# Windowed attention and two gated layers: block 1 keeps block 0's two PSUM pools, and the shared ring of four banks opens one block later

## Chip, cores and metric

One core of one Trainium2 chip. The metric is the device time of a run in microseconds (us); lower is better. A run counts by the median of several.

## What is computed

```python
scores = (1/sqrt(64)) * q @ k.T                    # 4 batches, 8 heads, 576 positions, head size 64
mask   = (rel >= 0) & (rel < 64)                   # each position sees itself and the 63 before it
x      = softmax(where(mask, scores, -1e9)) @ v    # -> 2304 tokens x 512
h      = x @ w_in                                  # 512 -> 2048
y      = gate(h) @ w_out                           # 2048 -> 512
h2     = y @ w_in2                                 # 512 -> 1024
out    = layernorm(h2 * softmax(h2)) * g_ln @ w_out2   # 1024 -> 512
```

## The kernel before

The tokens go in six blocks of 384 (`NBLK`). In each block the first layer runs over 16 feature slices `f` of 128. For one slice `moe_h` (L496) makes `ps_h` with 12 matmuls of 384 columns (four chunks of the model width, three products each, since every operand is split into a high and a low part), ACT and DVE make the gated value in two parts (L505, L506, L511, L512, L515), and two steps later `moe_y` (L526) adds it to four accumulators `acc` with 12 more matmuls. At a block's end `moe_out` copies the accumulators to `xo` (L536 on ACT, L538 on DVE) and POOL stores them (L539).

Between these steps stands the attention of the next block, cut into pieces that `slot()` takes from the generator `slots()`, one or two in each step. Up to the start of block 1 a piece treats a group of two heads: `st_s` makes scores (L352, with masked maximum on DVE at L360 and exponential on ACT at L366), `st_norm` divides (L377 to L386), `st_t` transposes the weights (`ps_p`, L400 and L402, copied out on ACT at L405 and L407), `st_v` multiplies with v (`ps_x`, L421, taken out at L428 and L429). From the group pair `PU` on a piece treats four heads: `pair_s` fills two score banks (L442, with L452 and L458 behind it), then two transposed banks, and `pair_v` one bank `ps_x` (L476, L483, L484). The pieces of block 1 make the input of block 2, and so on.

PSUM has eight banks. Four hold the accumulators. The other four belong, up to the end of block 0, to two pools of two: `ps_at` for the attention's tiles and `ps_h` for the slices. Then both are closed and one pool of four, the ring, gives its banks in turn to whoever asks, attention or slice (`at_bank`, `h_bank`). The loop over `seq` near the end (L850 on) writes the program step by step, and there the switch is made. The kernel is recorded with a scheduler that reorders instructions within each engine, so the order on an engine follows from the dependences that the banks leave, not from the text alone.

```python
    def h_bank():
        if ring:
            return ring[0].tile([128, 512], F32, tag="r", name="ps_h")
        return ps_h.tile([128, 512], F32, tag="h", name="ps_h")
```

Of the kernel before, what the change touches and what calls it, by code (L numbers as in the profile page):

```python
# [20 lines left out]
def kernel(  # L21
# [73 lines left out]
    def at_bank(name):  # L95
        if spare:
            spare.append(spare.pop(0))
            if spare[-1] is not None:
                return ps_acc.tile([128, 512], F32, tag=spare[-1], name=name)
        if ring:  # L100
            return ring[0].tile([128, 512], F32, tag="r", name=name)
        return ps_at.tile([128, 512], F32, tag="a", name=name)
# [47 lines left out]
    def w_conv(start=True):  # L150
        if w_b:
            split_c(*w_b.pop(0))
        if w_a:
            w_b.append(w_a.pop(0))
            split_b(*w_b[-1])
        if w_raw and start:
            w_a.append(w_raw.pop(0))
            split_a(*w_a[-1])
# [72 lines left out]
    def w2_vals(k):  # L231
        for y, a in (("B1", 0), ("B2", 2)):
            z = d_p.tile([128, 2, 512], F32, tag="st", bufs=4, name="w2v")
            for c in range(2):
                nc.sync.dma_start(out=z[:, c, :], in_=w2d[2 * (k + a) + c])
                w2v[f"{y}{c + 1}", k] = z[:, c, :]

    def w2_sums(k):
        for tag, a, b in (("e", "T1", "T2"), ("s", "T3", "T4")):
            z = d_p.tile([128, 2, 512], F32, tag=tag, bufs=3, name="w2t")  # L240
            w2v[a, k], w2v[b, k] = z[:, 0, :], z[:, 1, :]
        for y, a, b in (("T1", "B12", "B11"), ("T2", "B22", "T1"), ("T3", "B22", "B12"), ("T4", "B21", "T2")):
            nc.gpsimd.tensor_tensor(w2v[y, k], w2v[a, k], w2v[b, k], op=ALU.subtract)
# [246 lines left out]
    def moe_h(j, f, c):  # L490
        ps = h_bank()[:, c]
        n = 0
        for kc in range(KC):
            hi, lo = wih[f][:, kc, :], wil[f][:, kc, :]
            for a, bb in ((hi, xh[j]), (hi, xl[j]), (lo, xh[j])):
                nc.tensor.matmul(ps, a, bb[:, kc, c], start=(n == 0), stop=(n == 3 * KC - 1))  # L496
                n += 1
        return ps

    def moe_g(part, ps):  # L500
        c = part[2]
        u = wk_p.tile([128, NB], F32, tag="u", name="u")[:, c]
        hi = wk_p.tile([128, NB], F32R, tag="gh", bufs=3, name="gh")[:, c]
        lo = wk_p.tile([128, NB], F32R, tag="gl", bufs=3, name="gl")[:, c]
        nc.scalar.activation(u, ps, ACTF.Relu, bias=half, scale=0.5)  # L505
        nc.scalar.activation(u, u, ACTF.Square)  # L506
        gh[part[0], part[1], part[2].start], gl[part[0], part[1], part[2].start] = hi, lo
        return ps, u, hi, lo

    def moe_g2(ps, u, hi, lo):  # L510
        g = nc.vector.scalar_tensor_tensor(u, u, 1.0, ps, op0=ALU.min, op1=ALU.max)  # L511
        return nc.scalar.copy(hi, u).ins, g.ins  # L512

    def moe_g3(j, ps, u, hi, lo):
        nc.vector.tensor_tensor(lo, u, as_f32(hi), op=ALU.subtract)  # L515


    def moe_y(j, f, c):
        if f == 0 and c.start == 0:
            for e in range(KC):  # L520
                acc[j, e] = ps_acc.tile([128, 512], F32, tag=f"acc{e}", bufs=1, name=f"acc{e}")
        hi, lo = gh.pop((j, f, c.start)), gl.pop((j, f, c.start))
        for e in range(KC):
            wh, wl = woh[f][:, e * 128:(e + 1) * 128], wol[f][:, e * 128:(e + 1) * 128]
            for n, (a, bb) in enumerate(((wh, hi), (wh, lo), (wl, hi))):
                nc.tensor.matmul(  # L526
                    acc[j, e][:, c], a, bb,
                    start=(f == 0 and n == 0 and c.start == 0), stop=(f == NF - 1 and n == 2),
                )

    def moe_out(j, es):
        for e in es:
            xo = wk_p.tile([128, NB], F32, tag="u" if j == NBLK - 1 and e > 1 else "xo", name="xo")
            a = acc.pop((j, e))[:, 0:NB]
            if e % 2 == 0:
                nc.scalar.copy(xo, a)  # L536
            else:
                nc.vector.tensor_copy(xo, a)  # L538
            nc.gpsimd.dma_start(out=x2d[j][e], in_=xo)  # L539
# [9 lines left out]
    def w_load(n=1):  # L549
        for _ in range(n):  # L550
            if wq:
                w_raw.append(w1_unit(*wq.pop(0)))
# [96 lines left out]
    def slot(n):  # L649
        for _ in range(n):  # L650
            next(stages, None)
# [7 lines left out]
    def x2_load(p):  # L659
        r = x2r[p] = d_p.tile([128, KC, 256], F32, tag="x2", bufs=2, name="x2r")  # L660
        c = 0
        while c < 256:
            j, c0 = divmod(256 * p + c, NB)
            n = min(256 - c, NB - c0)
            nc.sync.dma_start(out=r[:, :, c:c + n], in_=x2d[j][:, :, c0:c0 + n].rearrange("e p n -> p e n"))
            c += n
# [171 lines left out]
    def l2_norm(m):  # L838
        ln_pins.append(st_ln(m))
        st_move(m)  # L840
# [9 lines left out]
    for n in range(len(seq) + 2):  # L850
        if n < len(seq):
            j, f, c = seq[n]
            last = j == NBLK - 1
            n0 = n1 = 1
            if c == FIRST:
                z = na * (f + 1) // F0 - na * f // F0
                n0, n1 = z - z // 2, z // 2
            if j == 1 and f == 0:
                fr_ctx.close()
                ring.append(rg_ctx.enter_context(  # L860
                    tc.tile_pool(name="ps_ring", bufs=4, space=PSUM, reuse_waits="tile")
                ))
            if last and f == 8:
                rg_ctx.close()
                ring[0] = ps_ctx.enter_context(tc.tile_pool(name="ps_ring2", bufs=2, space=PSUM, reuse_waits="tile"))
            if last and f == 0:
                at_ctx.close()
                d_p = ctx.enter_context(tc.tile_pool(name="d", bufs=2, side="right", reuse_waits="tile"))
                x2_load(0)
            if j == 1 and f == 4:  # L870
                gl_row = wk_p.tile([128, NB], F32, tag="xo", name="gl_row")[0:DF2 // 128, 0:128]
                nc.sync.dma_start(
                    out=gl_row.rearrange("k (b i) -> k b i", b=4),
                    in_=g_ln.rearrange("(b k i) -> k b i", b=4, i=32),
                )
            if j == 1 and f == 7:
                ps = at_bank("ps_g")
                nc.tensor.transpose(ps[:, 0:DF2 // 128], gl_row, ident[0:DF2 // 128, 0:DF2 // 128])
                nc.vector.tensor_copy(gl_sb, ps[:, 0:DF2 // 128])
            part = moe_g(seq[n], moe_h(j, f, c))  # L880
        if n >= 1 and n - 1 < len(seq):
            moe_g3(seq[n - 1][0], *prev)
        if n < len(seq):
            prev = part
            slot(n0)
            w_conv()
            pins = moe_g2(*part)
        if n >= 2:
            jy, fy, cy = seq[n - 2]
            moe_y(jy, fy, cy)  # L890
            if fy == NF - 1:
                moe_out(jy, (0, 1))
        if n < len(seq):
            slot(n1)
            w_conv()
            if j == 0:
                w_load(2)
            w2_step(n, *pins)
            if last and f < 2:
                w2_vals(f)  # L900
            if last and f in (2, 3):
                w2_sums(f - 2)
            if last and f >= 2:
                with tc.issue_after(pins[0]):
                    w2_split(f - 2)
            if last and 2 <= f < 10:
                w2_load(f - 2)
        else:
            w_conv()
        if n >= 2 and fy == NF - 1:  # L910
            moe_out(jy, (2, 3))
        if n < len(seq):
            if last and f == 1:
                x2_load(1)
            if last and f == 5:
                with tc.issue_after(pins[0]), tc.issue_after(pins[1]):
                    x2_prep(0)
            if last and f in P_STEPS:
                st_p(0, P_STEPS[f])
            if last and f == 14:  # L920
                l2_norm(0)
            if last and f == 15:
                st_p(1, "P2")
        elif n == len(seq):
            x2_load(2)
            x2_prep(1)
            st_p(1, "P3")
            l2_norm(1)
# [66 lines left out]
```

## Time and profile before

| | |
|---|---|
| median of 3 runs | 703.74 us (703.43 to 706.93) |
| profiled execution: its own time | 703.17 us |
| profiled execution: span from first to last instruction | 701.4 us |
| PE (matmul) busy | 678.1 us, 97% of the span |
| PEld (weight load) busy | 625.6 us, 89% |
| DVE busy | 448.3 us, 64% |
| ACT busy | 412.5 us, 59% |
| POOL busy | 134.2 us, 19% |

The span lies within the execution's own time, 1.8 us less. Busy time of PE counts overlapping matmuls once, and ends of matmuls are modelled, so a busy PE can still be slowed. The granted clock of TensorE is 0.998 of full speed over the span.

### The profile page before, as it was taken

Reading aid. Unit: us, or ns where it says so; the run is one execution under the profiler, and the core shown is the slowest. Engines: PE = TensorE matmul, PEld = TensorE weight load, DVE = VectorE, ACT = ScalarE, POOL = GpSimd, SP = SyncE. Lnnn points to the kernel's source line nnn. Section 1 sums busy time; section 2 is a strip of 40 time slices with the busy share of each in tenths; the row PEclk is TensorE's granted clock in tenths of the full one; section 3 lists DMA queues with packets and bytes.
Section 4 is the critical chain, followed back from the end, with each engine's and each line's share of the span. In section 5 each row is a group of like instructions: output and inputs, shape, how many; then the busy total and the mean of one; then the engine's idle time right before and its main releaser. Section 6 shows DMA issues by size and latency. Waiting matters only on the chain.

```text
span 701.4 us, 12574 instructions
## 1 busy us (share of the span) xinstructions
PE 678.1 (97%) x4439; PEld 625.6 (89%) x4439; DVE 448.3 (64%) x1213; ACT 412.5 (59%) x1006; POOL 134.2 (19%) x178
## 2 busy tenths in 40 slices
PE   6899888899999999999999999999999999999998
PEld 5689788799999999999999999999997888888887
DVE  4789889646445555454455552643289999999850
ACT  5889777665656655665566565364455555445451
POOL 1112221100001000021112111662272322220000
PEclk9999999999999999999999999999999999999999
DMA  9996896625353523346351211562024455444331
GB/s 194 253 241 161 218 245 196 148 35 108 72 116 112 116 64 76 77 129 126 85 113 61 106 41 51 173 202 93 1 83 142 155 178 189 158 147 150 103 109 46
DMA packets 150551, 88.94 MB, mean 127 GB/s; under 512 B 118616, under 2 KB 134744, under 8 KB 150488
## 3 DMA queue, kind: packets, MB, share of 16 engines
q1 hardware_dynamic: 135160, 49.84, 30.2%
q0 software_dynamic: 12592, 33.57, 14.9%
q10 hardware_dynamic: 2736, 4.72, 1.8%
q8 instruction: 35, 0.57, 0.3%
q14 instruction: 28, 0.23, 0.1%
HBM read 63.97 MB, written 24.12 MB: 126 GB/s over the span
## 4 chain that ended last, share of the span: by engine, by line
PE 71%; issue 13%; POOL 4%; DVE 4%; DMA 3%; SPq 3%; ACT 2%; POOLq 0%; DVEq 0%
PE acc L526 21%; PE ps_h L496 21%; PE ps_o L827 14%; PE P L712 9%; DMA wst<-in_moe_w_in_dram 3%; POOL wil L249 2%; PE ps_x L476 2%; PE ps_s L442 2%; PE ps_p L402 2%; SPq L279 1%; DVE gl L515 1%; POOL wst L124 1%; SPq L302 1%; POOL wst L126 1%; DVE x2p L692 1%
## 5 line engine op out<-in xcount | busy, mean ns | idle before, releaser
L511 DVE SCALAR_TENSOR_TENSOR u<-u,ps_h 128x384 f32<-128x384 f32 (+1 forms) x98 | 53.3, 544 | 142.3 <-ACT u L506 141.4
L496 PE MATMUL ps_h<-xh,wih 128*128 128x384 f32 (+1 forms) x392 | 132.0, 337 | 3.1 <-ACT wih L145 3.0
L526 PE MATMUL acc<-gl,woh 128*128 128x384 f32 (+1 forms) x392 | 130.3, 334 | 2.1 <-DVE gl L515 2.1
L496 PE MATMUL ps_h<-xl,wih 128*128 128x384 f32 (+1 forms) x392 | 130.7, 334 | 0.4 <-DVE xl L429 0.4
L496 PE MATMUL ps_h<-xh,wil 128*128 128x384 f32 (+1 forms) x392 | 130.9, 334 | 0.0
L526 PE MATMUL acc<-gh,wol 128*128 128x384 f32 (+1 forms) x392 | 129.3, 332 | 0.0
L526 PE MATMUL acc<-gh,woh 128*128 128x384 f32 (+1 forms) x392 | 123.8, 341 | 2.3 <-ACT gh L512 2.3
L505 ACT ACTIVATE u<-ps_h,half 128x384 f32<-128x384 f32 (+1 forms) x98 | 56.1, 574 | 97.5 <-PE ps_h L496 97.3
L515 DVE TENSOR_TENSOR gl<-u,gh 128x384 fp32r<-128x384 f32 (+1 forms) x98 | 62.6, 640 | 35.2 <-ACT gh L512 34.6
L512 ACT CAST gh<-u 128x384 fp32r<-128x384 f32 (+1 forms) x98 | 49.7, 508 | 49.9 <-DVE u L511 34.8
L496 PEld LDWEIGHTS ps_h<-xh,wih 128*128 128x128 f32 x392 | 74.1, 189 | 4.5 <-ACT wih L145 3.6
L526 PEld LDWEIGHTS acc<-gh,woh 128*128 128x128 f32 x392 | 72.0, 188 | 6.2 <-ACT gh L512 3.5
L526 PEld LDWEIGHTS acc<-gl,woh 128*128 128x128 f32 x392 | 73.7, 188 | 3.1 <-DVE gl L515 2.7
L496 PEld LDWEIGHTS ps_h<-xl,wih 128*128 128x128 f32 x392 | 74.1, 189 | 1.0 <-DVE xl L429 0.8
L496 PEld LDWEIGHTS ps_h<-xh,wil 128*128 128x128 f32 x392 | 74.1, 189 | 0.1
L526 PEld LDWEIGHTS acc<-gh,wol 128*128 128x128 f32 x392 | 73.6, 188 | 0.1
L712 PE MATMUL P<-wih,x2p 128*128 128x512 f32 x216 | 71.6, 390 | 0.7 <-DVE x2p L692 0.7
L827 PE MATMUL ps_o<-woh,wol 128*128 128x512 f32 (+1 forms) x152 | 57.6, 379 | 0.0
L827 PE MATMUL ps_o<-woh,woh 128*128 128x512 f32 (+1 forms) x152 | 57.5, 379 | 0.0
L827 PE MATMUL ps_o<-wol,woh 128*128 128x512 f32 (+1 forms) x152 | 57.5, 378 | 0.0
L506 ACT ACTIVATE u<-u 128x384 f32<-128x384 f32 (+1 forms) x98 | 51.1, 522 | 1.9
L712 PEld LDWEIGHTS P<-wih,x2p 128*128 128x128 f32 x216 | 40.4, 188 | 9.2 <-DVE x2p L692 1.1
(123 smaller groups left out, 1191.8 us busy)
## 6 DMA issues: line engine op xcount, KB each, us to landing
wst<-in_moe_w_out_dram POOLq DMA_DIRECT2D x22, 512.0 KB, 7.4
wst<-in_moe_w_in_dram POOLq DMA_DIRECT2D x21, 512.0 KB, 5.5
vw<-in_v_dram SPq DMA_DIRECT2D x32, 256.0 KB, 5.3
lnd<-e SPq DMA_DIRECT2D x16, 512.0 KB, 2.7
lT<-lnd SPq DMA_DIRECT2D x64, 128.0 KB, 3.0
x2d<-xo POOLq DMA_DIRECT2D x24, 192.0 KB, 2.6
out_dram<-o ACTq DMA_DIRECT2D x17, 256.0 KB, 2.0
w2d<-w2st POOLq DMA_DIRECT2D x8, 512.0 KB, 3.0
```

What stands on the lines that cost most here:

```text
L249: nc.gpsimd.tensor_tensor(lo, v_, as_f32(hi), op=ALU.subtract)
L402: nc.tensor.transpose(ps[:, i * 128:i * 128 + 128], p[:, i, :], ident)
L442: nc.tensor.matmul(ps[x][64 * c:64 * c + 64, i * 128 + c0:i * 128 + 128], z[r, KQ + i * 64:KQ + i * 64 + 64], z[r, i * 64 + c0:i * 64 + 12 ...
L496: nc.tensor.matmul(ps, a, bb[:, kc, c], start=(n == 0), stop=(n == 3 * KC - 1))
L505: nc.scalar.activation(u, ps, ACTF.Relu, bias=half, scale=0.5)
L506: nc.scalar.activation(u, u, ACTF.Square)
L511: g = nc.vector.scalar_tensor_tensor(u, u, 1.0, ps, op0=ALU.min, op1=ALU.max)
L512: return nc.scalar.copy(hi, u).ins, g.ins
L515: nc.vector.tensor_tensor(lo, u, as_f32(hi), op=ALU.subtract)
L526: nc.tensor.matmul(acc[j, e][:, c], a, bb, start=(f == 0 and n == 0 and c.start == 0), stop=(f == NF - 1 and n == 2),)
L712: nc.tensor.matmul(ps, l, r, start=(n == 0), stop=(n == 5))
L827: nc.tensor.matmul(ps, a[kk // 4][:, kk % 4, :], b[kk][:, c:c + w], start=(n == 0), stop=(n == 3 * NK2 - 1),)
```

## The change

The condition at which the two pools are closed and the ring is opened names block 2 in place of block 1. For the 16 slices of block 1, slices take turns on two banks of their own, and the attention of that block on two others.

```diff
-            if j == 1 and f == 0:
+            if j == 2 and f == 0:
                 fr_ctx.close()
                 ring.append(rg_ctx.enter_context(
                     tc.tile_pool(name="ps_ring", bufs=4, space=PSUM, reuse_waits="tile")
                 ))
```

No instruction is added or taken away. The orders of all engines agree up to the end of block 0 and again from the third slice of block 2 on. What moves stands between.

**First place: PE where block 0 ends.** `acc_753` and `acc_754` are block 0's last accumulations, `wih_146` and `wil_147` the weights of block 1's slice 0, `wih_168` and `wil_169` those of slice 1, `wih_176` of slice 2. Before:

```order
L526 MATMUL acc_753<-gh,wol_1409 128x384
L526 MATMUL acc_754<-gl,woh_1408 128x384
L526 MATMUL acc_754<-gh,wol_1409 128x384
L352 MATMUL ps_s<-kq_124 128x128 x3
L421 MATMUL ps_x<-pT,vw 64x64 x6
L402 MATMUL ps_p<-ident,p 128x128 x3
L352 MATMUL ps_s<-kq_125 128x128 x3
L496 MATMUL ps_h<-xh,wih_146 128x384
L496 MATMUL ps_h<-xl,wih_146 128x384
```

Now, in two pieces that follow each other:

```order
L352 MATMUL ps_s<-kq_124 128x128 x3
L421 MATMUL ps_x<-pT,vw 64x64 x6
L496 MATMUL ps_h<-xl,wih_146 128x384
L496 MATMUL ps_h<-xh,wil_147 128x384
L496 MATMUL ps_h<-xl,wih_168 128x384
L496 MATMUL ps_h<-xh,wil_169 128x384
L526 MATMUL acc_753<-gh,wol_1409 128x384
L526 MATMUL acc_754<-gl,woh_1408 128x384
L526 MATMUL acc_754<-gh,wol_1409 128x384
L496 MATMUL ps_h<-xh,wih_146 128x384
L496 MATMUL ps_h<-xh,wih_168 128x384
```

```order
L496 MATMUL ps_h<-xl,wih_146 128x384
L496 MATMUL ps_h<-xh,wil_147 128x384
L496 MATMUL ps_h<-xl,wih_168 128x384
L496 MATMUL ps_h<-xh,wil_169 128x384
L402 MATMUL ps_p<-ident,p 128x128 x3
L352 MATMUL ps_s<-kq_125 128x128 x3
L496 MATMUL ps_h<-xh,wih_176 128x384
```

Thirteen matmuls of 384 columns now stand between `ps_x` and `ps_p` where none stood; slices 0 and 1 of block 1 are begun earlier still and end here.

**Second place: PE in the middle of block 1, one visit of the attention.** `wil_857` belongs to slice 8, `woh_787` to slice 7. Before, twelve `ps_x` and both score banks (twelve matmuls) stand in one run:

```order
L496 MATMUL ps_h<-xh,wil_857 128x384
L476 MATMUL ps_x<-pT,vw 64x64 x12
L442 MATMUL ps_s<-kq_124 64x128 x2
L442 MATMUL ps_s<-kq_125 64x128 x2
L442 MATMUL ps_s<-kq_124 64x128 x2
L442 MATMUL ps_s<-kq_125 64x128 x2
L442 MATMUL ps_s<-kq_124 64x128 x2
L442 MATMUL ps_s<-kq_125 64x128 x2
L526 MATMUL acc_2047<-gh,woh_787 128x384
```

Now one of the twelve `ps_x` stands alone within slice 10, and eleven with one score bank (six matmuls) within slice 9's accumulation; the other score bank's six come 24 rows later:

```order
L496 MATMUL ps_h<-xh,wih_1034 128x384
L476 MATMUL ps_x<-pT,vw 64x64
L496 MATMUL ps_h<-xl,wih_1034 128x384
L496 MATMUL ps_h<-xh,wil_1035 128x384
L496 MATMUL ps_h<-xh,wih_1034 128x384
```

```order
L526 MATMUL acc_2044<-gh,woh_929 128x384
L476 MATMUL ps_x<-pT,vw 64x64 x11
L442 MATMUL ps_s<-kq_124 64x128
L442 MATMUL ps_s<-kq_125 64x128
L442 MATMUL ps_s<-kq_124 64x128
L442 MATMUL ps_s<-kq_125 64x128
L442 MATMUL ps_s<-kq_124 64x128
L442 MATMUL ps_s<-kq_125 64x128
L526 MATMUL acc_2044<-gl,woh_929 128x384
```

One visit has become three.

**Third place: ACT where block 1 begins.** L505 and L506 are the first two steps of a slice's gate. Before, the copy of the transposed weights (L407) and the exponentials (L366) come ahead of slice 0's gate:

```order
L536 COPY xo<-acc_753 128x384
L407 COPY pT<-ps_p 128x384
L366 ACTIVATE p,sm<-p,mx 128x128 x3
L505 ACTIVATE u<-ps_h,half 128x384
L428 CAST xh<-ps_x 128x192
L506 ACTIVATE u<-u 128x384
```

Now:

```order
L536 COPY xo<-acc_753 128x384
L505 ACTIVATE u<-ps_h,half 128x384 x2
L506 ACTIVATE u<-u 128x384 x2
L407 COPY pT<-ps_p 128x384
L512 CAST gh<-u 128x384
L366 ACTIVATE p,sm<-p,mx 128x128 x3
```

The gates of slices 0 and 1 stand together, the first step of both ahead of the second of either.

## Rows read from the trace of the kernel before

**Rows 1.** Busy time by stretch: window, length, PE, PEld, DVE, ACT, POOL, clock, DMA.
```profile
125.00:140.00 15.00, 12.61 (x109) 11.23 (x110) 8.82 (x30) 8.19 (x27) 2.73 (x5) 1.00 0.72 171
140.00:205.00 65.00, 65.00 (x522) 62.91 (x518) 35.58 (x121) 38.64 (x106) 3.26 (x6) 1.00 0.40 86
205.00:300.00 95.00, 95.00 (x742) 91.91 (x741) 49.70 (x159) 56.38 (x153) 9.08 (x16) 1.00 0.38 88
300.00:440.00 140.00, 140.00 (x1062) 136.04 (x1061) 68.12 (x207) 84.74 (x211) 23.69 (x30) 1.00 0.35 91
```

**Rows 2.** Waits of PE, 125 to 440 us: total us, times, longest.
```profile
PE ps_p L402 <- DVE p L386: 2.4, 1, 2.4
```

**Rows 3.** PE in order of time, end of block 0: start, us, what, [idle before].
```profile
129.23 0.34 PE L526 MATMUL acc<-gh,wol 128*128 128x384 f32 x1
129.40 0.83 PE L352 MATMUL ps_s<-kq 128*128 128x128 f32 x6
130.16 0.71 PE L421 MATMUL ps_x<-pT,vw 64*64 64x64 f32 x12
133.23 0.52 PE L402 MATMUL ps_p<-ident,p 128*128 128x128 f32 x3 [2.35 <-DVE p L386]
133.58 0.83 PE L352 MATMUL ps_s<-kq 128*128 128x128 f32 x6
134.32 0.44 PE L496 MATMUL ps_h<-xh,wih 128*128 128x384 f32 x1
```

**Rows 4.** DVE and ACT in order of time, around that wait.
```profile
132.52 0.56 DVE L386 TENSOR_TENSOR p<-p,rs 128x384 f32<-128x384 f32 x1
...
133.78 0.48 ACT L407 COPY pT<-ps_p 128x384 f32<-128x384 f32 x1 [1.34 <-PE ps_p L402]
```

**Rows 5.** The chain that ended last, one piece of 12 matmuls.
```profile
238.34 2.08 PE ps_h L496 x12
```

**Rows 6.** PE in order of time: transposes between two slices.
```profile
267.60 0.33 PE L496 MATMUL ps_h<-xh,wil 128*128 128x384 f32 x1
267.77 0.81 PE L402 MATMUL ps_p<-ident,p 128*128 128x128 f32 x6
268.34 0.42 PE L526 MATMUL acc<-gh,woh 128*128 128x384 f32 x1
268.60 0.34 PE L526 MATMUL acc<-gl,woh 128*128 128x384 f32 x1
```

**Rows 7.** PE in order of time: one run of v products and scores.
```profile
272.42 0.34 PE L496 MATMUL ps_h<-xh,wil 128*128 128x384 f32 x1
272.69 0.92 PE L476 MATMUL ps_x<-pT,vw 128*64 128x64 f32 x24
273.54 0.89 PE L442 MATMUL ps_s<-kq 64*64 64x128 f32 x24
274.35 0.44 PE L526 MATMUL acc<-gh,woh 128*128 128x384 f32 x1
274.63 0.33 PE L526 MATMUL acc<-gl,woh 128*128 128x384 f32 x1
```

**Rows 8.** PE in order of time, block 0: six v products alone.
```profile
101.37 0.86 PE L526 MATMUL acc<-gh,woh 128*128 128x384 f32 x4
102.15 0.71 PE L421 MATMUL ps_x<-pT,vw 64*64 64x64 f32 x12
102.80 0.44 PE L526 MATMUL acc<-gl,woh 128*128 128x384 f32 x1
103.08 0.34 PE L526 MATMUL acc<-gh,wol 128*128 128x384 f32 x1
```

**Rows 9.** All engines in order of time: from a slice's last matmul to its gate.
```profile
144.82 0.33 PE L496 MATMUL ps_h<-xh,wil 128*128 128x384 f32 x1
...
145.19 0.58 ACT L505 ACTIVATE u<-ps_h,half 128x384 f32<-128x384 f32 x1 [0.30 <-PE ps_h L496]
...
146.36 0.56 DVE L511 SCALAR_TENSOR_TENSOR u<-u,ps_h 128x384 f32<-128x384 f32 x1
```

## The prediction, as it was written before the result

> **What bounds the kernel now.** I read the table by stretches first. From 140 to 440 us PE is busy for the whole of each stretch and the clock stands at 1.00, its upper level of 2.4 GHz; in the 15 us around the end of block 0 it is idle for 15.00 - 12.61 = 2.39 us [rows 1]. ACT and DVE are busy for little more than half of these stretches, so they cost nothing where PE does not wait for them. Next the waits of PE: over 125 to 440 us there is one, 2.4 us, at the transposes `ps_p`, for DVE's division L386 [rows 2]. Then PE in order of time at that place: after the scores and the v products of 129.40 and 130.16 it has nothing until 133.23, since the transposes need the divided weights of the very scores before them [rows 3]. And slice 0 of block 1 stands behind all this although its inputs do not: it starts at 134.32, just after ACT's copy of `ps_p` out of its bank, which takes 0.48 us from 133.78 [rows 3, 4]. The first bank that the ring gives out is the one `ps_p` used last.
>
> So the part of the program that the change touches, some 100 us, is bound by PE: by its stream of matmuls, and by one hole of 2.35 us. Outside it nothing in the order moves, and a shift there shifts the end: in the stretches up to 440 us PE has no idle time that could swallow it.
>
> **What the change takes away: the hole.** With banks of their own, slices 0 and 1 no longer stand behind `ps_p`. Thirteen of their and block 0's last matmuls now lie between `ps_x` and `ps_p` (first place of the order). A full run of 12 takes 2.08 us, 0.173 each [rows 5], so 13 take 2.26. From the start of the scores to the start of the transposes the chain over DVE and ACT takes 133.23 - 129.40 = 3.83 us, of which PE now idles 2.35 [rows 3]; with 2.26 of work, and the way in and out of the attention's matmuls (below), hardly anything is left: 0 to 0.4, I take 0.2.
>
> **What it adds there: a wait for a slice's bank.** With two banks, slice 2 must wait until DVE's L511 has read slice 0 out. That chain is seen in block 1: from the start of a slice's last matmul at 144.82 to the end of L511 at 146.36 + 0.56 it takes 2.10 us [rows 9]. In the new order of ACT the first step of slice 1's gate, 0.58 us [rows 9], comes in between (third place), which makes up to 2.68. After slice 0's last matmul PE has two more matmuls, three transposes and three scores before slice 2: from the start of that last matmul 3 x 0.173, then from 133.23 to 134.32 for the other six [rows 3], 1.6 us together. The wait is then 0.5 to 1.1 us; I take 0.8. With the 0.2 from above, 1.0 of the 2.35 us comes back, so the hole gives a gain of 1.35.
>
> **What it moves: the attention's matmuls are cut into more visits.** With two banks for the attention, the two score banks, the two transposed banks and the v products of a group of four heads can no longer stand in one run. Between the rows where the two orders part and meet again I count, on PE, the runs of attention between slice work. Runs of transposes alone rise from 5 to 11; runs that hold scores or products (or the one small transpose `ps_g`) from 9 to 17.
>
> The transposes' runs cost nothing extra: from the last slice matmul at 267.60 to the second one after them at 268.60 is 1.00 us; less two steps of 0.173 leaves 0.65 for six, 0.109 each, and a run of three costs half of that [rows 6].
>
> The others do cost. The step into `ps_x` is 272.69 - 272.42 = 0.27 in place of 0.173, and the second step after the scores 274.63 - 274.35 = 0.28 [rows 7]: 0.20 us a visit at the least. Six products alone in block 0 show more: their four matmuls at 101.37 put the last before them at 101.89, and 103.08 - 101.89 less two steps is 0.84 us [rows 8], where in a long run twelve take 273.54 - 272.69 = 0.85, or 0.43 for six [rows 7]: 0.41 us for the visit. Eight more visits at 0.20 to 0.41 are 1.6 to 3.3 us; I take 0.3 each, 2.4, since some of the new visits hold scores and some begin behind transposes, where the way in is free. PE is busy throughout here, so all of it lies on the path.
>
> The Trainium skill has a rule on this, in "TensorEngine Tiling (Array Packing)", Tiling Modes: a change of tiling mode drains the engine. The products and scores run on 128*64 and 64*64 tiles and the slices on 128*128 [rows 7], so each new visit would be two changes; if each waited out a matmul's full 0.33 us [rows 9] beyond its step, 0.32 a visit, the eight would cost 2.6 and the sum would be +1.25. The rows' sum stands without it.
>
> **What costs nothing.** POOL stores block 0's result ahead of one weight load in place of behind it, and DVE takes two copies of `xo` later: both engines have time (POOL is busy 2.73 of 15 us there, DVE 8.82 [rows 1]), and the accumulators' next use is covered by slices 2 and 3. If that cover went, the price would be one copy, about the 0.56 us that L386 takes for an operand of the same size [rows 4]. SP's queue keeps its order. Where the ring opens in block 2, no such hole should come up: by then each half of a pair's weights is divided and transposed before the slices of block 2 are due.
>
> **Sum.** -2.35 + 1.0 + 2.4 = +1.05 us. On the profiled execution, 703.17 us (span 701.4), that is 704.2. The median of the runs before is 703.74, 0.57 above this execution, and with it the sum would be 704.8; I give 704.5, the middle. Half a per cent, 3.5 us, is about what a measurement of this kernel can tell from no change: faster would be under 700.2, slower over 707.3.
>
> **Rivals.**
> *The visits are free*: the longer steps are an effect of the particular neighbours and are hidden when a visit is short. Against it, both visits that I looked at show them [rows 7, 8]. Then the hole's 2.35 us remain as gain, or 1.35 with the wait for slice 2: 700.8 to 701.8, within half a per cent.
>
> *Two banks are too few for the attention*: each score bank must be read by DVE before the next tile takes it, and PE comes back to `ps_p` before the weights are divided, four or five times in block 1. The chain is 3.83 us from the scores to the transposes [rows 3], and it decides where less than that stands between them: fewer than 22 slice matmuls at 0.173. In the new order I find 27 at the closest (in slices 9 and 10), 4.7 us, and more elsewhere. If DVE's and ACT's other work of a slice got in first and made the chain longer by a gate (2.10 us, [rows 9]), each of four groups would lose 3.83 + 2.10 - 4.7 = 1.2 us: +4.9 on top of the sum, 709.1. The Trainium skill's "Perfetto Trace Analysis", Optimizing Tensor Performance, speaks for this rival: independent groups should rotate through different PSUM banks, so that the reading out of one overlaps the next one's matmuls. No row of before shows two banks at this point of the program.
>
> *Half a score tile costs as much as a whole*: in the old order two score tiles are filled in turns, 24 passes in 274.35 - 273.54 = 0.81 us [rows 7]. If a tile by itself finds no partner to run beside, its six matmuls take the 0.81 of twelve; four pairs would lose 4 x 0.81 = 3.2 us: 707.4 from the profiled execution. Against it, the six still alternate between two operands (`kq_124`, `kq_125`), which write different halves of the bank. No row of before shows a tile alone.
>
> That the change does nothing is excluded: the order shows what it moves.
>
> **How the numbers follow.** My forecast 0.76; free visits 0.08; two banks too few 0.08; half tiles 0.08. The range takes the forecast's bounds: at the low end visits at 0.20 and no wait left, -2.35 + 1.6 = -0.75, or 702.4; at the high end visits at 0.41 and a hole as long as before, +3.3, or 706.5. I set 701.6 to 707.0: the low end takes in free visits with the wait for slice 2 (701.8), the high end the 0.57 us by which the median stands above the execution (706.5 + 0.57), and what is left out is most of the two dear cases. Slower than 707.3 takes the two-banks case and half of the half-tile case with little else: 0.11. Faster than 700.2 needs free visits and something that I do not see: 0.03. The same: 0.86.
>
> **What would show it.** In the profile after, PE's wait of 2.4 us at `ps_p` should be gone from the end of block 0 and a shorter one, about 0.8 us, stand before slice 2's first matmul, ended by DVE's L511. From there to the third slice of block 2 PE should show no wait, but more single runs of `ps_x` and `ps_s`, each with steps of 0.27 to 0.28 us at its edges. The third slice of block 2 should come about 1 us later, and everything after it be shifted by as much. I am wrong if it comes earlier (the visits or the wait are cheaper), if PE waits at `ps_p` or `ps_s` in block 1 (two banks are too few), or if the six scores of one tile take as long as twelve do now.

## Result, and the profile after

710.12 us (median of six runs, 708.98 to 713.11) against 704.16 for the kernel before: a ratio of 1.0075, 95% interval 1.0051 to 1.0100, so 5.3 us slower (3.6 to 7.0). The forecast was 704.5, the range 701.6 to 707.0, so it was wrong.

The profiled execution took 710.1 us with a span of 708.3. Set against the span before (701.4) that is 6.9 us, more than the medians differ. One step of ACT's gate of a slice, before the changed stretch and after it, shows where they arise. The first two lines are of the kernel before, the next two of the changed one (ACT in order of time):

```profile
124.34 0.58 ACT L505 ACTIVATE u<-ps_h,half 128x384 f32<-128x384 f32 x1
240.46 0.59 ACT L505 ACTIVATE u<-ps_h,half 128x384 f32<-128x384 f32 x1 [0.42 <-PE ps_h L496]
```
```profile
125.69 0.58 ACT L505 ACTIVATE u<-ps_h,half 128x384 f32<-128x384 f32 x1
247.41 0.58 ACT L505 ACTIVATE u<-ps_h,half 128x384 f32<-128x384 f32 x1 [0.42 <-PE ps_h L496]
```

The first step is 1.35 us late, in block 0, where both kernels run the same instructions: the granted clock was lower in this execution, 0.89 against 0.94 over 30 to 60 us and 0.95 against 1.00 over 90 to 125 us. From the second step on everything is shifted by 6.95 us. So the changed stretch took 6.95 - 1.35 = 5.6 us more, and that agrees with the medians.

Busy time by stretch of the changed kernel, columns as in [rows 1] and its first three stretches, then all waits of PE from 125 to 447 us:

```profile
125.00:140.00 15.00, 13.50 (x98) 12.48 (x97) 7.26 (x29) 8.28 (x27) 1.64 (x3) 1.00 0.48 107
140.00:205.00 65.00, 65.00 (x470) 60.88 (x469) 32.40 (x103) 36.00 (x97) 3.79 (x7) 1.00 0.33 76
205.00:300.00 95.00, 95.00 (x758) 90.65 (x760) 48.82 (x159) 55.03 (x151) 7.98 (x14) 1.00 0.45 98
```
```profile
PE ps_h L496 <- DVE u L511: 1.5, 1, 1.5
```

PE idles less than before (1.50 us in the first stretch, where it was 2.39 in [rows 1]) and waits once, at slice 2's bank, for DVE's L511, as forecast. The clock is 1.00 throughout (from 300 to 440 us too, where PE is busy all the time). The time was lost with PE busy. The hole at the end of block 0, in PE, ACT and DVE in order of time (compare [rows 3, 4]; the matmul at 136.03 is slice 0's last):

```profile
136.03 0.33 PE L496 MATMUL ps_h<-xh,wil 128*128 128x384 f32 x1
...
136.55 0.50 PE L402 MATMUL ps_p<-ident,p 128*128 128x128 f32 x3
136.89 0.83 PE L352 MATMUL ps_s<-kq 128*128 128x128 f32 x6
139.22 0.46 PE L496 MATMUL ps_h<-xh,wih 128*128 128x384 f32 x1 [1.50 <-DVE u L511]
```
```profile
136.74 0.48 ACT L536 COPY xo<-acc 128x384 f32<-128x384 f32 x1 [1.29 <-PE ps_h L496]
137.11 1.06 ACT L505 ACTIVATE u<-ps_h,half 128x384 f32<-128x384 f32 x2
138.05 0.94 ACT L506 ACTIVATE u<-u 128x384 f32<-128x384 f32 x2
```
```profile
138.61 0.56 DVE L511 SCALAR_TENSOR_TENSOR u<-u,ps_h 128x384 f32<-128x384 f32 x1 [2.16 <-ACT u L506]
```

The transposes wait no longer. But the gates of slices 0 and 1 stand together, two L505 and then two L506, and ACT begins them only at 137.11, after a copy of block 0's result; L511 ends at 139.17, and slice 2 follows at 139.22.

And here is one group of four heads in the middle of block 1 (PE in order of time), where a group of the kernel before has one run, 0.85 us of products and 0.81 us of scores [rows 7]:

```profile
186.31 0.34 PE L496 MATMUL ps_h<-xh,wih 128*128 128x384 f32 x1
186.57 0.33 PE L476 MATMUL ps_x<-pT,vw 128*64 128x64 f32 x2
186.83 0.45 PE L496 MATMUL ps_h<-xl,wih 128*128 128x384 f32 x1
187.12 0.34 PE L496 MATMUL ps_h<-xh,wil 128*128 128x384 f32 x1
...
189.12 0.91 PE L476 MATMUL ps_x<-pT,vw 128*64 128x64 f32 x22
189.96 0.87 PE L442 MATMUL ps_s<-kq 64*64 64x128 f32 x12
190.76 0.45 PE L526 MATMUL acc<-gl,woh 128*128 128x384 f32 x1
...
195.13 0.87 PE L442 MATMUL ps_s<-kq 64*64 64x128 f32 x12
195.94 0.45 PE L526 MATMUL acc<-gl,woh 128*128 128x384 f32 x1
```

The trace holds two records for each of these small matmuls, so x12 is the six of one score tile. They take 190.76 - 189.96 = 0.80 us, and the other tile's six 195.94 - 195.13 = 0.81: each as long as all twelve in [rows 7]. Of the twelve products one has gone ahead alone: from 186.31 to 187.12 are 0.81 us, less two steps of 0.173 leaves 0.46 for it, and the other eleven take 0.84, about what twelve did (0.85).

The same reckoning for every run of attention between the two L505 above, from the slice matmul ahead of a run to the second one behind it, less two steps (us; the transposes and `ps_g` of a group are with it, and the first row goes up to the first group of four heads):

```
                                  before   after
end of block 0, start of block 1    7.19    6.61   -0.58
first group of four heads           1.52    2.51   +0.99
second                              2.88    4.13   +1.25
third                               2.52    3.99   +1.47
fourth                              2.42    3.77   +1.35
fifth                               2.87    3.86   +0.99
sum                                19.40   24.87   +5.47
```

That is 5.5 of the 5.6 us. The last five rows are 6.05: tiles filled alone 3.7 (three pairs of tiles at 0.80 + 0.80 - 0.82, two, with shorter matmuls, at 0.70 + 0.70 - 0.71), three lone products 1.4, and the rest, about 0.9, is put down to the remaining new visits.

### The profile page after: what moved, and what is told of

It reads as the page before. It is cut to its first block, busy times and chain, and to the rows that moved or that the text cites. A ratio compares the mean times of both kernels' runs of the same rounds, so it can differ in the third digit from the quotient of the medians.

```text
span 708.3 us, 12575 instructions
## 1 busy us (share of the span) xinstructions
PE 688.6 (97%) x4439; PEld 633.3 (89%) x4439; DVE 446.9 (63%) x1213; ACT 412.3 (58%) x1006; POOL 134.5 (19%) x178
## 4 chain that ended last, share of the span: by engine, by line
PE 74%; issue 13%; POOL 4%; DVE 4%; DMA 2%; ACT 2%; SPq 0%; POOLq 0%; DVEq 0%
PE acc L526 21%; PE ps_h L496 21%; PE ps_o L827 14%; PE P L712 9%; POOL wil L249 2%; PE ps_x L476 2%; PE ps_s L442 2%; PE ps_p L402 2%; PE ps_s L352 2%; DVE gl L515 1%; POOL wst L124 1%; PE ps_x L421 1%; DMA wst<-in_moe_w_out_dram 1%; DMA wst<-in_moe_w_in_dram 1%; PE ps_t L334 1%
## 5 line engine op out<-in xcount | busy, mean ns | idle before, releaser
L511 DVE SCALAR_TENSOR_TENSOR u<-u,ps_h 128x384 f32<-128x384 f32 (+1 forms) x98 | 53.2, 542 | 134.9 <-ACT u L506 134.3
L526 PE MATMUL acc<-gh,woh 128*128 128x384 f32 (+1 forms) x392 | 122.3, 341 | 1.0 <-ACT gh L512 1.0
L505 ACT ACTIVATE u<-ps_h,half 128x384 f32<-128x384 f32 (+1 forms) x98 | 55.8, 572 | 94.5 <-PE ps_h L496 94.4
L506 ACT ACTIVATE u<-u 128x384 f32<-128x384 f32 (+1 forms) x98 | 50.8, 520 | 1.9
```

What stands on the lines that cost most here:

```text
L526: nc.tensor.matmul(acc[j, e][:, c], a, bb, start=(f == 0 and n == 0 and c.start == 0), stop=(f == NF - 1 and n == 2),)
```

## Experiments

Theory: a score tile alone costs PE what both in turns cost, and with two banks five pairs are split. Rivals: the visits are dearer than forecast, or two banks are too few.

**Tiles apart, and in turns (control).** In the kernel before, `pair_s` with another order, held by `issue_after`:

```diff
-        for i in range(QB):
+        mm = None
+        for x, i, c in [(x, i, c) for x in range(2) for i in range(QB) for c in range(2)]:
...
+                mm is None or es.enter_context(tc.issue_after(mm))
+                mm = nc.tensor.matmul(
```

The control has `for i ... for c ... for x in (1, 0)` in that list.

> The kernel before with its pools as they are; in each of the 15 pairs the six score matmuls of one tile come first and then the six of the other, in one run, so that no visit is added and no bank is given out otherwise. Theory (a score tile alone costs PE as much as both in turns, since only the two tiles, from different row halves, run beside each other): the 12 matmuls take about 1.5 to 1.6 us in place of 0.81, so 15 pairs add 10 to 12 us: about 714 to 716 us where before is 704. Rival (the changed kernel lost its time at the edges of the added visits, or for want of banks): 0.81 us for the 12 as before, and no change within 1 us.

> Control for the run with the tiles apart: the kernel before with the same rewritten loop and the same forced order, but the two tiles in turns. Both theories: 0.81 us for each pair's 12 matmuls, as before, and no change within 1 us of 704. If it is slower by several us, the forced order itself costs and the other run says nothing.

Apart: 708.43 us against 705.24, ratio 1.0046 (1.0030 to 1.0063), +3.2 us. In turns: 705.58, ratio 1.0003 (0.9982 to 1.0024). PE in order of time, apart:

```profile
258.38 1.15 PE L442 MATMUL ps_s<-kq 64*64 64x128 f32 x24
259.46 0.44 PE L526 MATMUL acc<-gh,woh 128*128 128x384 f32 x1
```

A pair takes 1.08 us here, 0.27 more than in turns, and 15 x 0.27 = 4.0 us lies in the interval (2.1 to 4.4). The direction is the theory's, the size a third of what I wrote: back to back, the second tile's matmuls start while the first tile's are still running. A tile that has slice matmuls on both sides, as in the changed kernel, has no such neighbour.

**Both row halves in each tile,** in the kernel before and in the changed one:

```diff
-                        ps[x][64 * c:64 * c + 64, i * 128 + c0:i * 128 + 128],
+                        ps[c][64 * x:64 * x + 64, i * 128 + c0:i * 128 + 128],
...
-                        o[x][0:n, i, 64 * c:64 * c + 64],
+                        o[c][0:n, i, 64 * x:64 * x + 64],
```

> The kernel before with the same other split of the scores over the tiles, its pools as they are and all 15 pairs whole: control. If row halves decide, each pair's 12 matmuls take 0.7 to 0.82 us as before, and the time is that of before within 1 us. If two matmuls that write the same bank stand in each other's way, each pair takes longer, up to 1.6 us, and 15 pairs add up to 12 us.

> The changed kernel with another split of a pair's scores over the two tiles: a tile takes one pair of heads from both row halves in place of both pairs of one row half, so that a tile alone has matmuls of both row halves. The amount of work is the same; four pairs are split over two visits in place of five (26 and 16 runs in place of 28 and 17). Theory (a split pair costs twice because the matmuls of one row half do not run beside each other): six alone take about 0.4 us in place of 0.80, the four pairs and the fifth that is whole give back 3.5 to 4.2 us: 705.5 to 706.5 where before is 704.5 and the changed kernel 709.5 to 710. Rival (the loss is of the visits and of two banks being too few): 709 or more. A second way to fail: matmuls that write one bank do not run side by side; then the ten whole pairs get slower too, and the time is above the changed kernel's.

In the kernel before: 714.12 us against 704.35, ratio 1.0135 (1.0107 to 1.0164), +9.5. In the changed one: 714.80, ratio 1.0156 (1.0128 to 1.0184), +11.0, slower than the changed kernel. That is the time of the "second way to fail", but its reason, that matmuls which write one bank do not run side by side, is not what the traces show. PE, a whole pair in the kernel before with this split, and a tile by itself in the changed kernel with it:

```profile
260.97 1.53 PE L442 MATMUL ps_s<-kq 64*64 64x128 f32 x24
262.43 0.44 PE L526 MATMUL acc<-gh,woh 128*128 128x384 f32 x1
```
```profile
185.68 0.87 PE L442 MATMUL ps_s<-kq 64*64 64x128 f32 x12
186.49 0.44 PE L496 MATMUL ps_h<-xl,wih 128*128 128x384 f32 x1
```

A whole pair now takes 1.46 us, and 15 x (1.46 - 0.82) = 9.6 us is what was measured. But a tile by itself, whose six matmuls come from both row halves and write one bank, takes 0.81 us, as long as the six of one row half in the changed kernel. So writing one bank does not slow it.

What runs side by side can be read from the records. A matmul that stands alone leaves two records one behind the other (the lone score at 189.01 in the next experiment: 0.43 us from the start of the first to the end of the second, where one record takes 0.27 to 0.32). Records that start together therefore belong to different matmuls. Here are the records at the head of four runs of scores: a pair in the kernel before, a tile alone in the changed kernel, then a pair and a tile alone with the new split:

```profile
273.54 0.34 PE L442 MATMUL ps_s<-kq 64*64 64x128 f32 x4
```
```profile
189.96 0.33 PE L442 MATMUL ps_s<-kq 64*64 64x128 f32 x2
```
```profile
260.97 0.33 PE L442 MATMUL ps_s<-kq 64*64 64x128 f32 x2
```
```profile
185.68 0.33 PE L442 MATMUL ps_s<-kq 64*64 64x128 f32 x2
```

Four matmuls start together in a pair of the kernel before, two in each of the others. Each of them takes 64 rows and 64 columns, a quarter of the array. In the kernel before the row half goes with the tile (`x`) and the column half with the pair of heads (`c`): a pair of tiles uses all four quarters, a tile alone two of them. With the new split both halves go by `x`, so even a pair uses two quarters only, and takes nearly twice as long.

A further run keeps the tiles of the kernel before, and its four quarters, but lets two neighbours differ in row half, column half and bank: in the ordered loop above, the kernel before with

```diff
+        for x, i, c in [(x, i, c ^ x) for i in range(QB) for c in range(2) for x in range(2)]:
```

> The kernel before with the scores of a pair in turns, but so that two neighbours differ in the row half, the column half and the bank: a matmul of the first tile's one pair of heads goes with one of the second tile's other pair. It tells why the run with both row halves in each tile was slow. If two matmuls stand in each other's way because they write one bank, these run side by side: 0.7 to 0.82 us for the 12, and the time of before. If two matmuls only run side by side on the same column half: about 1.46 us for the 12, and some 9 us more.

A single run, 705.1 us against a median of 704.08. PE:

```profile
178.93 0.89 PE L442 MATMUL ps_s<-kq 64*64 64x128 f32 x24
179.74 0.44 PE L526 MATMUL acc<-gh,woh 128*128 128x384 f32 x1
```

0.81 us, as in the kernel before. The run was meant to tell the bank from the column; it only rules out that neighbours need the same column half. The Trainium skill says in "TensorEngine Tiling (Array Packing)", Restrictions and Gotchas, that different row tiles can't access one PSUM bank at the same time. The trace does not agree: the matmuls of a tile of the new split write one bank, start in twos from different row halves, and six take 0.81 us.

**The changed kernel with the tiles in turns.** The control's loop in the changed kernel.

> The changed kernel, with two banks for the attention and two for h through block 1, but the score matmuls of a pair forced into turns: in the five pairs that the change had split, one matmul of the first tile stands alone and the other eleven come together when the second bank is free. The number of visits stays as in the changed kernel (27 and 17 against 28 and 17). Theory (half tiles cost as much as whole ones): the five pairs give back up to 5 x 0.8 us less the one matmul that stands alone, about 3 to 4 us: 706 to 707.5 us where before is 704 and the changed kernel 709.5. Rival (visits or too few banks are the whole cost): no gain over the changed kernel, 709 to 710. If the pairs' later start makes the weights late, PE waits at the transposes and the gain is smaller.

709.12 us, ratio to before 1.0064 (1.0040 to 1.0087): hardly a gain over the changed kernel. PE in order of time, one pair, and the place of a new wait; then busy time by stretch there:

```profile
189.01 0.43 PE L442 MATMUL ps_s<-kq 64*64 64x128 f32 x2
189.37 0.44 PE L496 MATMUL ps_h<-xl,wih 128*128 128x384 f32 x1
...
193.91 0.88 PE L442 MATMUL ps_s<-kq 64*64 64x128 f32 x22
194.72 0.45 PE L496 MATMUL ps_h<-xh,wil 128*128 128x384 f32 x1
```
```profile
214.78 0.41 PE L496 MATMUL ps_h<-xh,wih 128*128 128x384 f32 x1 [1.86 <-DVE mx L452]
...
216.12 0.52 PE L496 MATMUL ps_h<-xh,wih 128*128 128x384 f32 x1
```
```profile
215.00:222.00 7.00, 7.00 (x36) 6.55 (x36) 4.29 (x14) 4.15 (x15) 1.63 (x3) 0.76 0.75 182
```

The pair costs 0.36 + 0.81 = 1.17 us in place of 1.61, so five would give back about 2.2. Where the ring opens it was lost again: PE waited 1.86 us for a score bank to be read, and then ran at a granted clock of 0.76 over 7 us, where a slice matmul takes 0.52 us in place of 0.33. Not conclusive by its time.

**The changed kernel with scores first.** In `slots`, the scores ahead of the products:

```diff
+            if P < NPP:
+                pair_s(P)
             if P == PU:
                 st_v(GB + 1)
             else:
                 pair_v(P - 1)
             if P % NPR == 0:
                 v_ahead(2 * P)
-            if P < NPP:
-                pair_s(P)
```

> The changed kernel with a pair's scores written ahead of the v products in the step where both stand, so that the two banks of the attention go to the two score tiles first: three of the five split pairs are whole again, two stay split (two single runs of six each), and the v products stay in one run of 12 in place of 1 and 11. The two banks and the opening in block 2 stay. Theory (split pairs cost 0.7 to 0.8 us each, a single product ahead of its eleven 0.45, a visit 0.2): 3 x 0.79 and 4 x 0.45 come back, less 0.2 each for up to three products that now stand apart from the scores: 3.5 us less than the changed kernel, 706 to 707 where before is 704.5. Rival (two banks are too few however they are used: PE waits for scores to be read out, or the lower clock follows): 709 or more.

704.77 us against 704.47, ratio 1.0013 (0.9995 to 1.0031): 0.9 us slower than before where the changed kernel is 5.3 slower. Its waits of PE from 125 to 450 us, and one pair:

```profile
PE ps_h L496 <- DVE u L511: 1.7, 1, 1.7
```
```profile
177.60 0.89 PE L442 MATMUL ps_s<-kq 64*64 64x128 f32 x24
178.41 0.45 PE L526 MATMUL acc<-gh,woh 128*128 128x384 f32 x1
```

The pair is whole again, 0.81 us, as are two others; the first two stay split. Two banks, and the ring in block 2, as in the changed kernel; between the two L505 steps it takes 1.8 us more than before, where the changed kernel takes 5.6. Of the 3.8 us that came back, three pairs (0.78 + 0.69 + 0.69) and three lone products (0.46 each) make 3.5. So most of the loss was the split, not the want of banks. (I counted four lone products there; it was three.)

**Visits alone.** In the kernel before, the scores one step later:

```diff
-            if P < NPP:
-                pair_s(P)
             yield
             if P < NPP:
+                pair_s(P)
                 st_norm(P, 0)
```

> The kernel before, its pools as they are, with a pair's scores moved one step behind the v products that they follow now: in 13 places a matmul run of a slice comes between the two, so that the runs with scores or products rise from 20 to 33, with no pair of tiles split and the same banks. It prices the visits alone. If a visit costs 0.2 to 0.3 us, as taken in the prediction, it is 2.6 to 3.9 us slower than before: 707 to 708.5 where before is 704.5. Rival (visits are free, and the changed kernel lost all of it by the split pairs and the waits): within 1 us of before.

708.36 us against 704.08, ratio 1.0050 (1.0033 to 1.0067), +3.5. PE, one product run and the scores that stood behind it:

```profile
176.59 0.34 PE L496 MATMUL ps_h<-xh,wil 128*128 128x384 f32 x1
176.85 0.92 PE L476 MATMUL ps_x<-pT,vw 128*64 128x64 f32 x24
...
177.98 0.34 PE L526 MATMUL acc<-gl,woh 128*128 128x384 f32 x1
...
179.72 0.34 PE L526 MATMUL acc<-gh,wol 128*128 128x384 f32 x1
179.99 0.89 PE L442 MATMUL ps_s<-kq 64*64 64x128 f32 x24
...
181.09 0.34 PE L496 MATMUL ps_h<-xl,wih 128*128 128x384 f32 x1
```

Apart they take (177.98 - 176.59) + (181.09 - 179.72) - 4 x 0.173 = 2.07 us, in one run [rows 7] 2.21 - 0.35 = 1.86. A visit costs 0.20 us, the lower bound of the prediction; 13 of them are 2.6, within the interval (2.3 to 4.7). Visits are not free.

**Where the ring opens.** The kernel before with `if j == 1 and f == 2:`, and the same with the two lines that open `ps_at` and `ps_h` (L88 and L89) exchanged.

> The ring of four is opened at slice 2 of block 1 in place of slice 0: slices 0 and 1 use the h banks and fill the hole at the end of block 0, and from slice 2 on the attention has four banks again, so no pair is split (15 runs of 12) and the visits are 16 and 9 in place of 14 and 9. Theory (the hole is worth 2.35 us less a wait for slice 2's bank, and what the change lost came later, from split tiles and more visits): 1 to 2 us faster than before, 702 to 703 where before is 704. Rival (the opening of the ring costs as much wherever it is, because the ring's banks must come free): 704 or more, with a new wait of PE at slice 2.

> The ring opened at slice 2 of block 1 as in the run above, and the two pools of block 0 opened in the other order, so that the first bank that the ring gives out is one of h (slice 0's, long read out) and not the one that the last score tile is written to; the order of the instructions stays. Theory (that run lost its time at the opening of the ring: 1.4 us of PE waiting for the scores' bank, and the lower clock that followed the idle time): PE's wait for L452 at slice 2 is gone, 1.4 us or more less than that run, about 706 to 708. Rival (the bank is not the cause, the attention's chain is): the wait moves to the next matmul that needs it, 709 to 711.

The first: 710.82 us against 705.24, ratio 1.0076 (1.0047 to 1.0106), where I expected a gain. The second: 705.66 against 704.35, ratio 1.0018 (1.0000 to 1.0036). The longest waits of PE, 125 to 450 us, of the first, with a stretch behind them (PE, then the others, as in [rows 1]), and of the second:

```profile
PE ps_x L421 <- ACT pT L407: 2.4, 2, 1.8
PE ps_h L496 <- DVE mx L452: 1.4, 1, 1.4
```
```profile
150.00:157.00 7.00, 6.76 (x23) 6.79 (x24) 2.88 (x11) 2.59 (x9) 0.00 (x0) 0.55 0.29 47
```
```profile
PE ps_x L421 <- ACT pT L407: 2.0, 2, 1.4
```

Behind the opening every pair is whole, yet the hole comes back at the opening itself: too little lies between transposes and the products that need them (2.4 us). And the ring's first bank is the first bank of the pool opened first: with `ps_at` ahead, the one that the pair's last score tile was just written to. With the exchange the wait for L452 is gone, and with it a stretch at 0.55 of the clock, near its lower level of 1.2 GHz.

**Block 0's copies.** The changed kernel with `if e % 2 == 0 and j:` in `moe_out`.

> The changed kernel with block 0's copies of its result all on DVE, so that ACT has none of them ahead of slice 0's gate. If PE's wait of 1.5 us at slice 2's bank was 0.7 longer than forecast because ACT's copy stands before that gate, it falls to about 0.8 us, and the rest of the stretch stays as in the changed kernel. Rival (the gate itself is the price): 1.4 to 1.5 us as before, or DVE's copies make the divided weights late and PE waits at the transposes instead.

A single run, 710.33 us. The wait for L511 is gone; another is there:

```profile
PE ps_p L402 <- DVE p L386: 1.3, 1, 1.3
```

ACT now begins slice 0's gate 0.37 us after the start of that slice's last matmul, as in [rows 9], but the copy on DVE stands ahead of the division L386. So the copies hold up ACT's gate or DVE's weights, and the hole keeps 1.3 to 1.5 us.

**Versions that might beat both.** The pools exchanged and kept until slice 3: with both row halves in each tile and the copies on DVE; with the copies alone; and with neither.

> What the readings so far would make of it: the two pools of block 0 opened in the other order and kept until slice 3 of block 1 (three slices to fill the hole, no pair split after it, 18 and 10 runs of attention in place of before's 14 and 9), the scores split over the tiles as in the run with both row halves in each tile, and block 0's copies of its result all on DVE, so that ACT comes sooner to the gate for which slice 2's bank waits. Theory: the hole's 2.35 us go, 0.8 come back at slice 2's bank, 0.6 for more visits: 1 us faster than before, 703 to 704 where before is 704.5. Rival (a new wait at the ring's opening, as in the run at slice 2): 706 or more.

> The last attempt at a version that beats both, with the scores over the tiles as they were: the two pools of block 0 opened in the other order and kept until slice 3 of block 1, and block 0's result copied by DVE alone. In its sister with the other split of the scores all else is the same, and each of the 15 pairs took 0.64 us more. Theory: 15 x 0.64 = 9.6 us less than that one's 714, 704.4, and by its trace (block 1 without the pairs' price 1.5 us shorter than before) 703 to 704, where before is 704.5. Rival (the two sets of runs don't add up so): 705 or more.

> The last version without the copies on DVE: the two pools of block 0 opened in the other order and kept until slice 3 of block 1, ACT and DVE sharing block 0's copies as before. Theory (the copies on DVE made the divided weights late by as much as they spared at slice 2's bank): PE waits 1.1 to 1.6 us at slice 2's bank and not at the transposes, in all 0.5 to 1 us less than the run with the copies on DVE: 703 where before is 704.5. Rival: no difference to that run, 703.5 to 704.5.

713.98 us (ratio 1.0126, 1.0100 to 1.0153), 703.73 (0.9984, 0.9967 to 1.0001) and 705.12 (1.0004, 0.9987 to 1.0022). The first shows the 0.64 us of each of its 15 pairs again. The other two can't be told from the kernel before. In the second PE waits 2.1 us at the transposes. In the last PE waits 1.3 us at slice 2's bank, 1.0 less than before, but its first pair of score tiles runs one after the other, 1.68 us in place of 0.82, and the gain is gone. None beats before by more than the measurement can tell.

## Why the prediction was wrong

*The step that failed* is the price of a split pair of score tiles, which the sum put at nothing. It stood there as the rival "half a score tile costs as much as a whole", priced rightly (0.81 us a pair) and given 0.08. I argued against it that the six "still alternate between two operands (`kq_124`, `kq_125`), which write different halves of the bank". That is so, and those two do run side by side; but in the old order four ran at once. A tile alone fills two quarters of the array in place of four, and its six take 0.80 us, what twelve took. [rows 7] gave the time of the twelve and I didn't ask how many of them it held at once. Five pairs, not four, were split: 3.7 us. With it the sum would have been +4.75 (1.05 + 3.7), near the 5.6 of the trace; most of the rest is the wait at slice 2's bank.

*The hole* went from the transposes, as forecast, with thirteen matmuls in front of them and no wait left there (0.2 was taken). *The wait for slice 2's bank* was 1.5 us in place of 0.8: one step of slice 1's gate came in between, as counted. But ACT began slice 0's gate at 137.11, 1.08 us after the start of that slice's last matmul, where [rows 9] have 0.37: a copy of block 0's result stood ahead of it. That copy itself began only at 136.74, after 1.29 us without work; what it waited for isn't settled. So 0.85 us were won, and 0.27 of it went to new visits at that place.

*The visits* came to about what was taken, 2.4, but by two errors that cancel. A visit costs 0.20, not 0.3; but a single product ahead of its eleven costs 0.46, since the eleven take as long as the twelve. That the two cancel was luck. The 0.3 leaned on a way in that is free behind transposes, which no run shows: at 165.5 us of the changed kernel three transposes and a lone product behind them take 0.79, no less than three transposes (0.33) and a lone product (0.46) apart. The prediction's 0.32, for two waits of a full matmul, is more than the 0.20 measured. Transposes alone were free, as forecast.

*Two banks are too few* was rightly doubted as worded: PE never waits for a score bank or for the weights in block 1 of the changed kernel. What they cost was that they cut what belongs together.

## What to carry to other kernels

Small matmuls that share the array are worth something only in company: before a change of banks or pools, ask of every run of them how many run at once, and whether the new order still brings as many together, in different quarters of the array. Count the split of such a group by the time of the whole group, not by its number of instructions. When a pool has too few banks for all tiles of a step, the order in which the step asks for them (scores first, then products) may be worth more than another bank.

## What the runs showed of the hardware

Matmuls of 64 rows and 64 columns ran side by side when they used different quarters of the array: four at once in a pair of tiles (0.81 us for twelve), two at once in a tile alone (0.80 us for six), and as fast when the two came from different row halves and wrote one bank (0.81). Twelve over two quarters took 1.46 us. No run here has all four quarters writing one bank.

The hole of before can cost more than its idle time. After the same idle 2.35 us the granted clock stayed at 1.00 in two profiles (before, and the tiles in turns), and over 130 to 140 us it was 0.83 in four others of kernels with that hole. PE in the one with the tiles apart:

```profile
134.65 0.88 PE L402 MATMUL ps_p<-ident,p 128*128 128x128 f32 x3 [2.35 <-DVE p L386]
...
136.46 0.67 PE L496 MATMUL ps_h<-xh,wih 128*128 128x384 f32 x1
```

From the transposes to slice 0 this takes 1.81 us, in [rows 3] 134.32 - 133.23 = 1.09.
